# Expert rows loaded and turned in two tiles of half the turn's width, and the first pair's nearness products written five times over

## The chip, the cores and the metric

The kernel runs on one core of one Trainium2 chip. Each time is the device time of one execution in microseconds (us). The kernel before was run three times without a profile (764.43, 764.62 and 766.75 us, median 764.62) and once with one.

## The reference

Three stages follow each other, all in float32, over 1536 tokens of 512 numbers (2 batches of 768, 8 heads of 64):

```
q_assign = argmax(q_n . c_n);  k_assign = argmax(k_n . c_n)     # 16 centroids a head, unit vectors
attn     = softmax(q k^T / 8, only where q_assign == k_assign) @ v
x        = heads side by side, 1536 x 512
e        = argmax(xn . en / tau)          # one of 8 experts for each token
x        = gate * (relu(x @ w1[e]) @ w2[e])        # w1: 512 x 1024, w2: 1024 x 512
out      = ((x @ w_a) * (x @ w_b)) @ w_out         # 512 -> 1536 -> 512
```

## The kernel before, in words

**Attention** works on eight pairs of heads (four a batch), twelve steps a pair: `scores` (L620, L621) makes a 128 x 768 block of scores, `rowmax` (L629) its maximum on VectorE, `expo` (L634) the exponential on ScalarE, `etrans` (L652) turns the block on TensorE, `pv_gen` (L679) multiplies it with v. The cluster mask is a part of the scores' product: `prep_gen` finds each row's cluster and writes it as 16 further rows of the scores' operands `Q3` and `K3`.

**The first pair's preparation** (`prep_gen(0)`) has nothing to hide behind, since no scores can run before it. For head 0 it turns q and k (`turned`, L437), multiplies them with the 16 centroids in high and low halves, 32 columns for each tile of 128 rows (`near_c`, L449), adds the halves up on VectorE (L450), finds the maxima in a chain of VectorE instructions that ends with the one-hot tile `oh` (L491), and turns `oh` on TensorE (L554, tile `t2`), in three groups of four, between which the same products for head 1 stand (L449 again, six in each of two places). `near_c` runs for pair 0 alone; later pairs use `near_all` (L457). While TensorE would stand still there, `keep_warm` (L273) puts products of ones into a bank that nobody reads: six of 512 columns (`FL1`) stand ahead of the first group of L554. The instructions of an engine run in the order in which the code issues them; each engine waits for others by semaphores.

**Experts** (`layer1`, `layer2`). A scatter has put the rows of each expert into its own part of `xs_d` in HBM. There are eight turns, one an expert, with fixed widths (`WIDTHS` 256, 160, 256, 224, 248, 216, 192, 176): so many rows are computed in a turn. Turn 0 is gathered on the chip as the attention ends. For the turns 1 to 7 `load_xe` (L1194) fetches 256 rows, whatever the width, on ScalarE's DMA queue, as two tiles of 128 rows by 512, and `trans_x` (L1213) turns them with eight transposes of 128 columns into two PSUM banks, of which the first `WIDTHS` columns are copied out (L1218, L1222, L1224). A turn has eight blocks; `load_xe(e + 2)` is issued behind block 5 of turn e, and `trans_x(e + 1)` behind block 5 of turn e (block 6 in turn 0).

**Weights** stream all the while: `load_raw` (L159, SyncE's DMA queue) fetches 512 KB into one of four `raw` buffers, ScalarE rounds them (L210) and VectorE takes the rest (L213), which frees the buffer for the next fetch. ScalarE's casts stand in one queue with the relu of the blocks (L1309, L1316), so a cast that waits for its DMA holds the relu behind it.

**The last stage** (L1232, L1480) multiplies with `w_a`, `w_b` and `w_out`; neither part of the change touches it.

Of the kernel before, what the change touches and what calls it, by code (L numbers as in the profile page):

```python
# [9 lines left out]
F32 = mybir.dt.float32  # L10
# [12 lines left out]
P = 128  # L23
FAR = float(2.0 ** 100)
CAP = 256
WIDTHS = (256, 160, 256, 224, 248, 216, 192, 176)
# [17 lines left out]
FL6 = 3  # L44
STAND = {8: 4}
FL1 = 6
FL2 = 2
FL3 = 5

# [2 lines left out]
def kernel(  # L52
# [15 lines left out]
    nc = tc.nc  # L68
    B, H, S, D = q.shape
# [13 lines left out]
    CT = CAP // P  # L83
# [16 lines left out]
    xs_d = dram.tile([NE * RX, DM], F32, name="xs_d")  # L100
# [157 lines left out]
    identr = left.tile([P, P], F32R, name="identr")  # L258
# [11 lines left out]
    def keep_warm(ps, n):  # L270

        for _ in range(n):
            nc.tensor.matmul(ps.rearrange("p (a b) -> p a b", b=P), ones, ones.rearrange("p (o c) -> p o c", o=1).to_broadcast([P, 4, P]), start=True, stop=True)  # L273
# [40 lines left out]
    cbuf = att.tile([P, H, 7 * 2 * C], F32R, name="cbuf", bufs=1)  # L314
    own = slice(3 * 2 * C, 4 * 2 * C)
# [94 lines left out]
    def prep_gen(pp):  # L410

        a, c = rows_hl.pop(pp)
        Q2 = att.tile([P, 2 * S], F32R, tag="Q2", name=f"Q2_{pp}")
        K2 = att.tile([P, 2 * S], F32R, tag="K2", name=f"K2_{pp}")
# [4 lines left out]
        hp = pp % HP  # L419

        def bank(dt, name):
            return psa.tile([P, 512], dt, tag="rot", name=name, bufs=3)
# [17 lines left out]
        def near_c(hs, t0, t1, sv):  # L440
            slots = [2 * h + isk for h in hs for isk in range(2)]
            ns = len(slots)
            w = 2 * C
            pt = bank(F32, f"sm_{pp}_{t0}")
            for t in range(t0, t1):
                for i, sl in enumerate(slots):
                    h, isk = divmod(sl, 2)
                    o = ((t - t0) * ns + i) * w
                    nc.tensor.matmul(pt[:, o:o + w], (Q2, K2)[isk][:, h * S + t * P:h * S + (t + 1) * P], cbuf[:, 2 * hp + h, own], start=True, stop=True)  # L449
            nc.vector.tensor_reduce(out=sv[:, t0:t1].rearrange("p t s c -> p (t s) c"),  # L450
                                    in_=pt[:, :(t1 - t0) * ns * w].rearrange("p (a z c) -> p a c z", z=2, c=C), axis=AX.X, op=ALU.add)

# [52 lines left out]
        if pp == 0:  # L505
            for h in range(2):
                for dst, src in ((K2, c), (Q2, a)):
                    for g0 in (h * NT, h * NT + HALF):
                        turned(dst, src, g0, g0 + HALF)
                        if h:  # L510
                            next(firsts[0][3], None)
                        yield
                dup(slice(h * S, (h + 1) * S))
                svs[h] = new_sv((h,))
                if h == 0:
                    near_c((h,), 0, NT, svs[h])
                    first_of(h)
                    yield
# [17 lines left out]
        for hs, ns, ohs, fg in firsts:  # L536
# [5 lines left out]
            if pp == 0:  # L542
                h = hs[0]
                order = [(1, t) for t in range(NT)] + [(0, t) for t in range(NT)]
                for u in range(0, len(order), 4):
                    if h == 0 and u:
                        near_c((1,), (0, HALF)[u > 4], (HALF, NT)[u > 4], svs[1])
                    elif h == 0:
                        keep_warm(wps[:, :512], FL1)
                    pt = bank(F32, f"t2_{pp}_{u}")  # L550
                    if h:
                        keep_warm(pt, FL2 if u else FL3)
                    for j, (isk, t) in enumerate(order[u:u + 4]):
                        nc.tensor.matmul(pt[D:D + C, j * P:(j + 1) * P], oh[:, t, isk, :], identb, start=True, stop=True)  # L554
                    for isk in (1, 0):
                        js = [j for j in range(4) if order[u + j][0] == isk]
                        if not js:
                            continue
                        src = pt[D:D + C, js[0] * P:(js[-1] + 1) * P]
                        c0 = h * S + order[u + js[0]][1] * P  # L560
                        dst = (Q3, K3)[isk][D:, c0:c0 + len(js) * P]
                        if isk and u:
                            nc.scalar.activation(dst, src, AF.Copy, scale=FAR, bias=-FAR)
                        elif isk:
                            nc.vector.tensor_scalar(out=dst, in0=src, scalar1=-1.0, scalar2=FAR, op0=ALU.add, op1=ALU.mult)
                        else:
                            evac(dst, src)

                    if u + 4 < len(order):
                        yield  # L570
            elif pp == 1:
                R = ns * C
                ohT = att.tile([R, NT, P], F32R, tag="ohT", name=f"ohT_{pp}", bufs=1)
                pt = psa.tile([P, 1024], BF16, tag="rot", name=f"t2_{pp}", bufs=3)[:R, :NT * P]
                for j in range(NT):
                    nc.tensor.matmul(pt[:, j * P:(j + 1) * P], oh[:, j].rearrange("p s c -> p (s c)"), identb, is_transpose=True, start=(j == 0), stop=(j == NT - 1))
                src = pt.rearrange("p (b i) -> p b i", i=P)
# [5 lines left out]
            else:  # L583
                pt = bank(F32, f"t2_{pp}")[:, :NT * ns * C]
# [314 lines left out]
    for s in range(nst):  # L899
        g_, h, t = steps[s]  # L900
        pp = g_[0]
        i = s % SPP
# [6 lines left out]
        if s >= SPP and zeros:  # L909
            dst, src = zeros.pop(0)  # L910
# [150 lines left out]
    def new_x(key, dt=F32R):  # L1061
        return big.tile([P, 2, DC, CAP], dt, tag="xT", name=f"xT_{key}", bufs=2)
# [8 lines left out]
    key, cap, held, over, obase, pbase = (left.tile([P, 1, NE], F32, name=n) for n in ("key", "cap", "held", "over", "obase", "pbase"))  # L1071
# [119 lines left out]
    def load_xe(e):  # L1191
        t = big.tile([P, CT, DM], F32R, tag="xe", name=f"xe_{e}", bufs=2)
        at_row = nc.values_load(turn_i[0:1, NE + e:NE + e + 1], engines=[mybir.EngineType.Activation], min_val=RX, max_val=(NE - 1) * RX)
        i = nc.scalar.dma_start(out=t.bitcast(F32), in_=xs_d[bass.ds(at_row, CAP), :].rearrange("(c p) d -> p c d", p=P))  # L1194
        if e == 1:
            for o in scatters:
                tc.add_manual_dep(i.ins, o.name, DATA, reason="rows of every scatter")
        xe_t[e] = t
# [3 lines left out]
    def turn_bank():  # L1202
        ring[0] += 1
        return ("et0", "et1", "pp", "pv")[(ring[0] - 1) % 4]

    def trans_x(key, src):

        x = new_x(key, F32 if KINDS[key] == "one" else F32R)
        hi, lo = x[:, 0], x[:, 1]
        pts = [ps_t.tile([P, 2, CAP], F32R, tag=turn_bank(), name=f"xT_{key}_{u}") for u in range(2)]  # L1210
        for t in range(CT):
            for j in range(DC):
                nc.tensor.transpose(pts[j // 2][:, j % 2, t * P:(t + 1) * P], src[:, t, j * P:(j + 1) * P], identr)  # L1213
        pts = [p.bitcast(F32) for p in pts]
        wd = WIDTHS[key]
        if KINDS[key] == "one":
            for u in range(2):
                (nc.vector.tensor_copy if u else nc.scalar.copy)(hi[:, 2 * u:2 * u + 2, :wd], pts[u][:, :, :wd])  # L1218
            xT_t[key] = x
            return  # L1220
        for u in range(2):
            nc.scalar.copy(hi[:, 2 * u:2 * u + 2, :wd], pts[u][:, :, :wd])  # L1222
        for u in range(2):
            nc.vector.tensor_sub(lo[:, 2 * u:2 * u + 2, :wd], pts[u][:, :, :wd], hi[:, 2 * u:2 * u + 2, :wd])  # L1224
        xT_t[key] = x
# [273 lines left out]
    for G in range(total_f + tot + LAG):  # L1499
# [10 lines left out]
        if I < 0:  # L1510
            layer1(G)
            if G in (2, NF - 1):
                load_xe(1 if G == 2 else 2)
            if G == NF:
                further()
            if G == GR - 2:
                tc.mark_branch_hint_location("rare", "LikelyTaken", engines=[mybir.EngineType.DVE])
            e, f = divmod(G, NF)
            if 2 * NF <= G < 3 * NF:
                next(rr, None)  # L1520
            if G > 3 * NF:
                next(gg, None)
            if f == (5 if e else NF - 2):
                if e + 1 < NE:
                    trans_x(e + 1, xe_t[e + 1])
            if f == 5 and 0 < e < NE - 2:
                load_xe(e + 2)
        elif I < tot:
            bil1(I)
            next(pg_, None)  # L1530
# [52 lines left out]
```

## Time and profile before

| what | value |
|---|---|
| runs without a profile | 764.43, 764.62, 766.75 us |
| profiled execution | 765.42 us, of which the span from first to last instruction is 763.9 us |
| TensorE | busy 750.4 us, 98% of the span |
| VectorE, ScalarE | busy 464.3 us (61%) and 374.3 us (49%) |
| mean granted TensorE clock | 0.997 |

A share of the clock of 1.00 stands for 2.4 GHz, 0.50 for 1.2 GHz. "PEld" is the loading of the array's weights, which overlaps the products on "PE". A row of the timeline that ends in [x <-engine tile line] tells how long the engine stood idle before it and who released it.

### The profile page before, as it was taken

The numbers are of one execution on the slowest core, as the hardware profiler recorded it, in microseconds if no ns is written. First come the engines' busy times: TensorE is split into PE (matmuls) and PEld (weight loads), VectorE is DVE, ScalarE is ACT, GpSimd is POOL, SyncE is SP. The second block draws the span as 40 slices with busy tenths as digits, with TensorE's granted clock in tenths as the row PEclk, the third lists the DMA queues.
The fourth block names the chain that finished last, engine by engine and source line by source line (L and its number), as shares of the span: only waits on it lengthen the run. The fifth ranks groups of instructions, "written<-read, shape, count | busy, mean of one in ns | idle before, by whom it ended". The sixth has DMA issues, their size and how long they took to land.

```text
span 763.9 us, 12711 instructions
## 1 busy us (share of the span) xinstructions
PE 750.4 (98%) x4788; PEld 629.7 (82%) x4788; DVE 464.3 (61%) x912; ACT 374.3 (49%) x770; POOL 106.3 (14%) x145
## 2 busy tenths in 40 slices
PE   8999999999999999999999999999999999999996
PEld 5767777777777679998999999888898888888995
DVE  6877676787867677478876898677643121121211
ACT  4656766777676675366655565344332121111211
POOL 6303203051300041000000004122001020000201
PEclk9999999999999999999999999999999999999999
DMA  6327133161321026889879877554401010000100
GB/s 189 84 87 252 43 95 90 59 195 58 91 52 32 28 97 231 313 283 298 285 240 279 276 220 219 121 146 111 137 7 52 1 56 0 1 1 0 56 1 28
DMA packets 47747, 91.86 MB, mean 120 GB/s; under 512 B 6264, under 2 KB 19832, under 8 KB 47680
## 3 DMA queue, kind: packets, MB, share of 16 engines
q1 hardware_dynamic: 43472, 81.01, 35.5%
q0 software_dynamic: 2304, 6.31, 2.2%
q10 hardware_dynamic: 1904, 3.67, 1.4%
q8 instruction: 39, 0.64, 0.4%
q14 instruction: 28, 0.23, 0.1%
HBM read 69.27 MB, written 14.04 MB: 109 GB/s over the span
## 4 chain that ended last, share of the span: by engine, by line
issue 28%; PE 26%; DMA 3%; DVE 1%; POOL 1%; ACT 1%; POOLq 0%; SPq 0%; ACTq 0%; DVEq 0%
PE ab L1232 7%; PE y L1349 5%; PE y L1353 3%; PE h L1313 3%; PE h L1232 2%; DMA raw<-in_moe_w_dram 2%; PE h L1305 2%; PE o_sc L1480 1%; PE h L1314 1%; PE y L1354 1%; POOL out_dram L1458 1%; DVE w L213 1%; PE o_pp L1480 1%; PE o_pv L1480 1%; ACT w L210 1%
## 5 line engine op out<-in xcount | busy, mean ns | idle before, releaser
L1436 DVE TENSOR_TENSOR ga<-ab,ga 128x256 f32<-128x256 f32 (+1 forms) x48 | 26.7, 557 | 156.7 <-PE ab L1232 110.9
L634 ACT ACTIVATE E<-sc,nmx 128x768 f32<-128x768 f32 x96 | 86.8, 904 | 53.9 <-DVE nmx L629 46.7
L1232 PE MATMUL ab<-xT_b,w 128*128 128x256 f32 (+1 forms) x720 | 113.1, 304 | 0.0
L1232 PE MATMUL ab<-x,w 128*128 128x512 f32 x432 | 108.1, 390 | 0.0
L1232 PEld LDWEIGHTS ab<-xT_b,w 128*128 128x128 f32 x720 | 98.6, 190 | 7.2
L629 DVE TENSOR_REDUCE nmx<-sc 128x1 f32<-128x768 f32 x96 | 91.4, 953 | 6.8 <-PE sc L621 5.6
L1232 PEld LDWEIGHTS ab<-x,w 128*128 128x128 f32 x432 | 81.1, 188 | 17.2
L652 PEld LDWEIGHTS et<-ident,E 128*128 128x128 f32 x576 | 62.3, 140 | 32.4 <-ACT ET L656 12.8
L1435 ACT COPY ga<-ab 128x256 f32<-128x256 f32 (+1 forms) x48 | 23.1, 481 | 126.9 <-PE ab L1232 123.7
L652 PE MATMUL et<-ident,E 128*128 128x128 f32 x576 | 82.4, 279 | 1.6 <-ACT E L634 1.2
L658 DVE COPY ET<-et 128x384 f32<-128x384 f32 x96 | 52.6, 548 | 50.5 <-PE et L652 50.3
L620 PE MATMUL sc<-K,Q 80*128 80x512 f32 x192 | 73.0, 380 | 0.0
L679 PE MATMUL pv<-ET,v 128*64 128x384 f32 (+2 forms) x408 | 72.3, 479 | 0.3 <-DVE xrow L699 0.2
L213 DVE TENSOR_TENSOR w<-raw,w 128x1024 fp32r<-128x1024 f32 x48 | 58.1, 1218 | 19.3 <-ACT w L210 18.8
L1480 PE MATMUL o_sc<-w,g 128*128 128x512 f32 x288 | 69.5, 390 | 0.0
L1437 ACT CAST g<-ga 128x256 fp32r<-128x256 f32 (+1 forms) x48 | 24.7, 514 | 84.2 <-DVE ga L1436 84.2
L1480 PEld LDWEIGHTS o_sc<-w,g 128*128 128x128 f32 x288 | 53.9, 188 | 11.3
L621 PE MATMUL sc<-K,Q 128*128 128x512 f32 x192 | 61.3, 340 | 0.0
L1349 PE MATMUL y<-hh,w 128*128 128x256 f32 (+3 forms) x416 | 59.2, 290 | 0.0
L210 ACT CAST w<-raw 128x1024 fp32r<-128x1024 f32 x47 | 49.4, 1053 | 16.3 <-DMA raw<-in_moe_w_dram 12.3
L1349 PEld LDWEIGHTS y<-hh,w 128*128 128x128 f32 x416 | 54.4, 190 | 0.3 <-DVE ys L1323 0.3
L656 ACT COPY ET<-et 128x384 f32<-128x384 f32 x96 | 45.7, 476 | 2.7 <-PE et L652 2.7
(277 smaller groups left out, 1206.9 us busy)
## 6 DMA issues: line engine op xcount, KB each, us to landing
raw<-in_moe_w_dram SPq DMA_DIRECT2D x48, 512.0 KB, 5.1
w<-in_moe_w_dram SPq DMA_DIRECT2D x16, 512.0 KB, 9.7
raw<-in_moe_w_a_dram SPq DMA_DIRECT2D x12, 512.0 KB, 5.1
raw<-in_moe_w_b_dram SPq DMA_DIRECT2D x12, 512.0 KB, 4.5
raw<-in_moe_w_out_dram SPq DMA_DIRECT2D x12, 512.0 KB, 3.6
xs_d<-zero SPq DMA_DIRECT2D x8, 512.0 KB, 6.4
xe<-xs_d ACTq DMA_DIRECT2D x7, 512.0 KB, 6.5
v<-in_v_dram SPq DMA_DIRECT2D x8, 384.0 KB, 3.1
```

The source lines that it names most:

```text
L210: (nc.scalar.copy if late is None else nc.vector.tensor_copy)(hi, w)
L213: nc.vector.tensor_sub(lo, w, hi)
L620: nc.tensor.matmul(ps[:, lo:hi], Q3[:, qs], K3[:, h * S + lo:h * S + hi], start=True, stop=False)
L621: nc.tensor.matmul(ps[:, lo:hi], Q2[:, qs], K2[:, h * S + lo:h * S + hi], start=False, stop=True)
L629: nc.vector.tensor_reduce(out=nmx[pp][:, h, t:t + 1], in_=sc[s], axis=AX.X, op=ALU.max, negate=True)
L634: nc.scalar.activation(e, sc.pop(s), AF.Exp, bias=nmx[pp][:, h, t:t + 1], accum_out=sums[pp][:, t, h:h + 1])
L652: nc.tensor.transpose(pt[:, j * P:(j + 1) * P], e[:, kt * P:(kt + 1) * P], ident)
L658: nc.vector.tensor_copy(dst, src)
L679: nc.tensor.matmul(pv[h * D:(h + 1) * D, :], vt[:, h, kt, :], ets[g, h][:, kt, :n * P], start=(kt == 0), stop=(kt == NT - 1))
L1232: nc.tensor.matmul(ps, s_, m_, start=(i == 0), stop=(i == len(ops) - 1))
L1349: nc.tensor.matmul(ys_ps[e][j // 2][:, j % 2, :wd], w[:, m_, ff, j * P:(j + 1) * P], s_, start=(f == 0 and i == 0 and j % 2 == 0), stop=(l ...
L1480: nc.tensor.matmul(o_ps[ck][t], s_[:, t * P:(t + 1) * P], w_[:, m_], start=(f == 0 and i == 0), stop=(J == I and f == NF2 - 1 and i == 2))
```

## The change

`near_c`: each product writes 160 columns in place of 32, the same 32 five times side by side (`AGAIN`). The next product begins 32 columns further on and writes over the four copies, so that what L450 reads stays the same; the last one of a bank ends at column 512, the bank's end. There are 24 such products.

`load_xe` and `trans_x`: with h half the turn's width, the rows come as two tiles of h rows, 2 h in place of 256 rows, and the transposes take h rows by 128 and write h columns each. The h of the turns 1 to 7 are 80, 128, 112, 124, 108, 96 and 88.

```diff
+AGAIN = 5
...
-                    nc.tensor.matmul(pt[:, o:o + w], (Q2, K2)[isk][:, h * S + t * P:h * S + (t + 1) * P], cbuf[:, 2 * hp + h, own], start=True, stop=True)
+                    nc.tensor.matmul(pt[:, o:o + AGAIN * w].rearrange("p (a c) -> p a c", c=w), (Q2, K2)[isk][:, h * S + t * P:h * S + (t + 1) * P],
+                                     cbuf[:, 2 * hp + h, own].rearrange("p (o c) -> p o c", o=1).to_broadcast([cbuf.shape[0], AGAIN, w]), start=True, stop=True)
...
-        i = nc.scalar.dma_start(out=t.bitcast(F32), in_=xs_d[bass.ds(at_row, CAP), :].rearrange("(c p) d -> p c d", p=P))
+        h = WIDTHS[e] // CT
+        i = nc.scalar.dma_start(out=t[:h].bitcast(F32), in_=xs_d[bass.ds(at_row, CT * h), :].rearrange("(c p) d -> p c d", p=h))
...
+        h = WIDTHS[key] // CT
...
-                nc.tensor.transpose(pts[j // 2][:, j % 2, t * P:(t + 1) * P], src[:, t, j * P:(j + 1) * P], identr)
+                nc.tensor.transpose(pts[j // 2][:, j % 2, t * h:(t + 1) * h], src[:h, t, j * P:(j + 1) * P], identr[:h, :h])
```

No engine gets an instruction more or less, or another order; shapes change alone. On TensorE, in the first pair's preparation (sm is the tile of the nearness products, t the turned rows, wps the bank of the warming products), before:

```order
L449 MATMUL sm_0_235<-cbuf,Q_0_185 128x32
L449 MATMUL sm_0_235<-cbuf,K_0_186 128x32
...
L437 MATMUL t_0_6_253<-identr,kr_169 128x128 x3
L437 MATMUL t_0_9_261<-identr,kr_169 128x128 x3
L437 MATMUL t_0_6_268<-identr,qr_168 128x128 x3
L437 MATMUL t_0_9_274<-identr,qr_168 128x128 x3
```

and now, its lines numbered one or two higher:

```order
L451 MATMUL sm_0_235<-cbuf,Q_0_185 128x160
L451 MATMUL sm_0_235<-cbuf,K_0_186 128x160
...
L438 MATMUL t_0_6_253<-identr,kr_169 128x128 x3
L438 MATMUL t_0_9_261<-identr,kr_169 128x128 x3
L438 MATMUL t_0_6_268<-identr,qr_168 128x128 x3
L438 MATMUL t_0_9_274<-identr,qr_168 128x128 x3
```

Only the last number of the products moved, from 32 to 160.

On ScalarE's queue, behind block 5 of turn 2, where the rows of turn 4 are fetched between the casts of two weight buffers (hh is the relu, xT the turned rows of turn 3, w the rounded weights), before:

```order
L1222 CAST xT_5619<-xT_1_5621 128x2x224
L1194 DMA xe_5634<-xs_d 128x2x512
L210 CAST w_5594<-raw_5511 128x1024
L1309 ACTIVATE hh_5662<-h_5663 128x256
L210 CAST w_5690<-raw_5556 128x1024
```

and now:

```order
L1227 CAST xT_5619<-xT_1_5621 128x2x224
L1198 DMA xe_5634<-xs_d 124x2x512
L211 CAST w_5594<-raw_5511 128x1024
L1314 ACTIVATE hh_5662<-h_5663 128x256
L211 CAST w_5690<-raw_5556 128x1024
```

The transfer keeps its place and goes over 124 partitions in place of 128.

On TensorE, behind block 6 of turn 0, where turn 1 is turned, before and then now:

```order
L1232 MATMUL h_5113<-xT_3559,w_3623 128x256 x12
L1213 MATMUL xT_0_5129<-identr,xe_3654 128x128 x2
L1213 MATMUL xT_1_5130<-identr,xe_3654 128x128 x2
...
L1349 MATMUL y_0_3667<-hh_5030,w_3713 128x256 x2
L1349 MATMUL y_1_3668<-hh_5030,w_3713 128x256 x2
```

```order
L1237 MATMUL h_5113<-xT_3559,w_3623 128x256 x12
L1218 MATMUL xT_0_5129<-identr,xe_3654 128x80 x2
L1218 MATMUL xT_1_5130<-identr,xe_3654 128x80 x2
...
L1354 MATMUL y_0_3667<-hh_5030,w_3713 128x256 x2
L1354 MATMUL y_1_3668<-hh_5030,w_3713 128x256 x2
```

The eight transposes stand where they stood and write 80 columns each.

## Rows read from the trace of the kernel before

**Rows 1.** The page: busy us, share of the span and instructions of each engine.

```profile
PE 750.4 (98%) x4788; PEld 629.7 (82%) x4788; DVE 464.3 (61%) x912; ACT 374.3 (49%) x770; POOL 106.3 (14%) x145
```

**Rows 2.** TensorE's waits over the span: us in total, times, longest.

```profile
PE h L1232 <- DVE hh L1310: 1.7, 1, 1.7
```

**Rows 3.** Stretches: length, busy us (instructions) of each engine, PEclk, DMA share, GB/s.

```profile
5.00:9.00 4.00, 3.39 (x24) 1.82 (x22) 2.65 (x12) 2.47 (x8) 1.33 (x4) 1.00 0.95 294
9.00:10.30 1.30, 1.30 (x13) 1.30 (x13) 0.91 (x1) 0.36 (x1) 1.00 (x1) 1.00 0.86 173
11.70:14.30 2.60, 2.60 (x8) 0.69 (x6) 1.16 (x4) 2.25 (x4) 1.02 (x1) 0.50 0.77 182
```

**Rows 4.** Timeline of the preparation: start, us, engine, line, operation.

```profile
7.38 0.25 DVE L321 TENSOR_SCALAR csq<-cent_sb,c_r 128x64 f32<-128x64 f32 x1
7.78 0.44 PE L325 MATMUL pc<-ident,csq 128*64 128x128 f32 x4 [0.46 <-DVE csq L321]
11.68 2.73 PE L273 MATMUL wps<-ones 128*128 128x512 bf16 x6
12.68 0.36 DVE L491 TENSOR_TENSOR oh<-smm,mx 128x192 bf16<-128x192 f32 x1
14.34 0.60 PE L554 MATMUL t<-identb,oh 128*16 128x128 bf16 x4
15.75 0.39 PE L554 MATMUL t<-identb,oh 128*16 128x128 bf16 x4
16.84 0.39 PE L554 MATMUL t<-identb,oh 128*16 128x128 bf16 x4
18.68 1.90 PE L273 MATMUL kw<-ones 128*128 128x512 bf16 x8
```

**Rows 5.** Timeline: two products of 32 columns, two of 256 columns.

```profile
9.48 0.26 PE L449 MATMUL sm<-cbuf,K 128*128 128x32 f32 x1
9.60 0.26 PE L449 MATMUL sm<-cbuf,Q 128*128 128x32 f32 x1
...
17.74 0.28 PE L620 MATMUL sc<-K,Q 80*128 80x256 f32 x1
17.86 0.29 PE L621 MATMUL sc<-K,Q 128*128 128x256 f32 x1
```

**Rows 6.** Transposes: eight and what follows; weight loads by line, ns min/median/max.

```profile
304.94 0.80 PE L1213 MATMUL xT<-identr,xe 128*128 128x128 f32 x8
305.57 1.67 PE L1349 MATMUL y<-hh,w 128*128 128x256 f32 x12
L1213 PEld LDWEIGHTS xT<-identr,xe x56: 137/140/143, 304.8 to 431.0; 128*128 128x128 f32 x56
L376 PEld LDWEIGHTS pe__756<-ident,en x4: 132/137/138, 51.7 to 51.9; 8*128 8x128 f32 x4
```

**Rows 7.** Transfers: ScalarE's queue over the span; all packets from 0 to 30 us.

```profile
q10 hardware_dynamic: 1904, 3.67, 1.4%
DMA packets 2834, 4.01 MB, mean 134 GB/s; under 512 B 520, under 2 KB 2568, under 8 KB 2832
```

**Rows 8.** Stretches of the experts, columns as in rows 3.

```profile
321.00:324.00 3.00, 3.00 (x28) 3.00 (x27) 2.17 (x3) 2.90 (x5) 0.00 (x0) 1.00 0.47 150
357.00:360.00 3.00, 3.00 (x24) 2.92 (x23) 2.37 (x4) 1.99 (x6) 0.00 (x0) 1.00 0.91 307
```

**Rows 9.** Timeline around TensorE's one wait, and behind it.

```profile
347.89 1.05 ACT L210 CAST w<-raw 128x1024 fp32r<-128x1024 f32 x1 [1.55 <-DMA raw<-in_moe_w_dram]
348.85 0.38 ACT L1309 ACTIVATE hh<-h 128x256 fp32r<-128x256 f32 x1
350.58 1.69 PE L1232 MATMUL h<-xT,w 128*128 128x256 f32 x12 [1.68 <-DVE hh L1310]
358.13 0.39 DVE L1318 SCALAR_TENSOR_TENSOR hh<-hf,hh 128x224 fp32r<-128x224 f32 x1
360.20 0.37 PE L1353 MATMUL y<-hh,w 128*128 128x448 f32 x1
```

## The prediction

> **What bounds the kernel now.** I read the busy time of the engines first. TensorE is busy 98% of the span [rows 1]: time comes off where TensorE waits or where its work shrinks, and any work added in its queue may cost. Then TensorE's waits: one stands out, 1.68 us before a layer 1 product at 350.58 [rows 2, 9]. Last, the granted clock by stretches, since busy time hides a slow clock: 1.00 from 5 to 10.3 us, and 0.50 (1.2 GHz) from 11.7 to 14.3 [rows 3]. So there are three places to look at: the first 17 us, the seven turnings, and the weight stream about 350 us. The change puts wider products into the first, fewer columns into the second, and fewer rows but another cut of the transfer into the third.
>
> **The wide products, taken by themselves.** The 32-column products follow each other every 0.12 us (9.48, 9.60), and so do two of 256 columns (17.74, 17.86) [rows 5]: the time between two hardly depends on columns up to there, so 160 columns cost nothing, 24 times. Below nothing is excluded, since no instruction goes; above, the last one's columns could delay VectorE's sum behind it by some 0.05 us, three times. I take 0. No wait is added: SyncE's, ScalarE's and GpSimd's queues get nothing here.
>
> **What they may change is the clock.** Before it fell, TensorE had not stood still: it was busy 1.30 of 1.30 us from 9.0 to 10.3, with the twelve narrow products, against 3.39 of 4.00 in the stretch before, with transposes and 512-column products, behind which the clock had stayed [rows 3]. What differs is what ran, and the change makes five times the columns run there. The rows don't tell what the clock goes by; that it stays up now is my likeliest case and no more.
>
> If it stays, two pieces shorten. First, the six warming products ahead of the first group of L554: they start at 11.68 and take 2.73 us, so that L554 starts at 14.34, though the one-hot tile it needs is done at 12.68 + 0.36 = 13.04 [rows 4]. At the full clock eight of the same kind take 1.90 us, 0.24 each at most [rows 4]; six end their turn at 11.68 + 6 x 0.24 = 13.1, so what is late next is `oh`. From VectorE's end to TensorE's start the pair csq (7.63) and pc (7.78) has 0.15 us, which puts L554 at 13.04 + 0.15 = 13.19: 14.34 - 13.19 = 1.15 us sooner. Second, the first round of L554 and six nearness products takes 15.75 - 14.34 = 1.41 us, the second, the same work behind the clock's return, 16.84 - 15.75 = 1.09 [rows 4]: 0.32 us. Together -1.47. VectorE's next steps wait for TensorE there, so all of it moves up, the scores too; with TensorE at 98% afterwards, nothing behind takes it back. Ends: 0 (the clock falls just the same) and -1.5; I take -1.5.
>
> **The transposes.** Eight take 305.57 - 304.94 = 0.63 us, 0.079 each [rows 6]. Half a width is 80 to 128; the sum of (1 - h/128) over seven turns is 1.25. If time went with columns, the gain would be 1.25 x 0.63 = 0.79 us. If the weight loads set it, nothing: a load takes 140 ns with 128 rows and 137 with 8 rows [rows 6], so fewer rows don't shorten it. That excludes a loss too. The load row is the nearer one; I take -0.1.
>
> The Trainium skill has a rule here ("TensorE: Matmul & The Clock Gate", section "LDWEIGHTS (loading the stationary operand)"): a load takes the columns of the weights over 1.2 GHz, which for 128 columns is an estimate of 107 ns and would hide all that the moving side saves. The pairs here follow each other every 79 ns, under that figure, so the measurement decides and the loads aren't the whole of it. By that rule this term is 0, by the other end 0.79.
>
> **Fewer rows fetched.** 1472 in place of 1792 rows of 2 KB, 640 KB less. That can help only at the one stall: ScalarE's cast at 347.89 had waited 1.55 us for a weight buffer, the relu stood behind it until 348.85, and TensorE until 350.58 [rows 9]. Turn 1's transfer (192 KB less) comes long before, and in between, from 321 to 324, the DMA engines were busy for 0.47 only [rows 8], so its gain is spent. Turn 3's saves 64 KB; at 307 GB/s [rows 8] that is 0.2 us. Ends: 0 and the whole stall, -1.7. I take -0.2.
>
> **Another cut of the transfers.** ScalarE's queue has 1904 packets for seven transfers [rows 7], 272 each: 256 rows and 16 tails, one an engine, so 16 rows an engine. From 0 to 30 us 520 packets are under 512 B [rows 7]. The centroids and tau have 128 each, which leaves 264 tails for 17 transfers, 16 x 16 + 8: the one over 8 partitions (`emb_sb`) used 8 engines. So the cut is in equal whole shares. 80, 128, 112 and 96 partitions divide by 16; 124 divides at most by 4, 108 by 12, 88 by 11. Turn 4's transfer, issued right behind the cast at 347.89, would then put 248 / 4 = 62 rows on each of four engines, 46 more than now. A packet takes 763.9 x 16 x 0.014 / 1904 = 0.09 us [rows 7], so this is 46 x 0.09 = 4.1 us more on four engines, in a stretch where all are at 0.91 [rows 8] and a weight buffer is whole only when its slowest engine is done. What hides it: its own use comes a turn later, and if packets of the two queues alternate, a weight buffer's 16 packets there wait for 16 others, 16 x 0.09 = 1.4 us. The relu's second half ends at 358.52 and its product starts at 360.20 [rows 9], 1.7 us of cover. Turn 5's (18 rows an engine) adds 0.2 us under the same cover, turn 7's none. Ends: 0 and +4.1; I take +0.3.
>
> **Sum.** -1.5 - 0.1 - 0.2 + 0.3 = -1.5. The profiled execution took 765.42 us (span 763.9 and 1.5 around it), 0.8 over the median of 764.62; no row tells whether the runs without a profile had the same fall of the clock. I set the sum against the median: 763.1 us.
>
> **The rivals.**
> - *The clock falls all the same*, or fell only in the profiled execution. For: TensorE was wholly busy before the fall and it came. Against: the wide products are the one difference to the stretch before. Left are -0.1 - 0.2 + 0.3: 764.6.
> - *Turn 4's transfer holds the weight stream.* On four engines the weight packets stand behind the 62, not between them: 4.1 us late, less the cover of 1.7 is 2.4 us of TensorE's idle time about 355 to 362, and with it the castings queue up before the relu as at 347.89. It decides from 1.7 us of lateness on. With the startup's gain: 764.6 - 1.8 + 2.4 = 765.2, and 766.9 where no cover is left: slower than before. For: ScalarE already waits for weights there. Against: queues may alternate.
>  The Trainium skill states this cut ("DMA: Bandwidth & Descriptors", section "Why a DMA increments its semaphore by 16 and not by 1"): a transfer uses the largest number of engines up to 16 that divides the partitions. By that rule 124 go over 4; the trace agrees for 8 partitions, and none of before has 124.
> - *Both small terms come whole.* The transposes give 0.8 and the stall at 350.58 goes, 1.7: 764.6 - 1.5 - 0.8 - 1.7 = 760.6, with half of each 761.9. For: a load lasts 140 ns and a pair takes 79 [rows 6], so loads overlap and something else may set the pace. Against: the idle DMA engines from 321 to 324.
>
> **How the numbers follow.** What a measurement of this kernel can tell from no change is about 0.3%, 2.3 us: 762.3 and 766.9. Forecast 0.50, with a range of its own from 762.1 to 764.2; clock falls 0.22, stream held 0.14, small terms whole 0.14. Faster: the third rival and a fifth of the forecast, 0.14 + 0.10 = 0.24. Slower: half of the second rival, 0.07. Same: 0.69. The range leaves out the ends of the last two rivals: 761.7 to 765.7.
>
> **What would show it.** The clock at 1.00 from 11.7 to 14.3 and the first L554 near 13.2: right; at 0.50, the first rival. The nearness products still 0.12 us apart. Eight transposes of turn 1 under 0.55 us would mean that columns count. ScalarE's queue with 1472 rows and 16 x 4 + 4 + 12 + 11 = 91 tails, 1563 packets, would show the uneven cut, 1584 an even one. An idle time of TensorE between 352 and 362, released by VectorE, the second rival. The forecast is wrong if the median leaves 762.1 to 764.2, and its first step is wrong if the clock stays and the third group of L554 still starts at 16.84.

## The result, and the profile after

The changed kernel took 772.07 us (median of 6 runs, 770.18 to 773.85), the kernel before 764.52 beside it (6 runs, 762.90 to 766.75): a ratio of 1.0092, 95% interval 1.0077 to 1.0107. That is 7.5 us slower. The forecast was 763.1 with a range up to 765.7: it was wrong, and on the other side.

The page of the changed kernel: span, the engines' line (VectorE, ScalarE and GpSimd stand within 0.7 us of [rows 1]), and ScalarE's DMA queue with packets, MB and share.

```profile
span 771.4 us, 12709 instructions
PE 752.9 (98%) x4788; PEld 632.1 (82%) x4788; DVE 465.0 (60%) x912; ACT 374.2 (49%) x770; POOL 106.3 (14%) x145
q10 hardware_dynamic: 1563, 3.02, 1.3%
```

The share of TensorE is still 98%. The span went from 763.9 to 771.4, while its busy time grew by 2.5 us only, so some 5 us are idle time. The queue's 1563 packets are the count that the prediction gave for the uneven cut: 1472 rows and 91 tails.

TensorE's waits, with us in total, times, longest. They answer to [rows 2].

```profile
PE y L1358 <- DVE hh L1323: 3.5, 1, 3.5
PE h L1237 <- ACT xT L1138: 1.4, 1, 1.4
PE y L1358 <- ACT ys L1367: 0.9, 1, 0.9
PE h L1237 <- DVE hh L1315: 0.8, 1, 0.8
```

The wait of before, 1.7 us on `hh` at 350, is down to 0.8. A new one, 3.5 us in one piece, stands ahead of a layer 2 product of turn 3. Its place is read in the timeline (start, us, engine, line, operation, idle time before and its releaser); the lines answer to [rows 9].

```profile
348.72 0.52 ACTq L1198 DMA_DIRECT2D xe<-xs_d  x1
352.85 1.05 ACT L211 CAST w<-raw 128x1024 fp32r<-128x1024 f32 x1 [0.74 <-DMA raw<-in_moe_w_dram]
360.59 1.04 ACT L211 CAST w<-raw 128x1024 fp32r<-128x1024 f32 x1 [6.41 <-DMA raw<-in_moe_w_dram]
361.55 0.35 ACT L1321 ACTIVATE hh<-h 128x224 fp32r<-128x224 f32 x1
363.23 0.39 DVE L1323 SCALAR_TENSOR_TENSOR hh<-hf,hh 128x224 fp32r<-128x224 f32 x1
363.77 0.44 PE L1358 MATMUL y<-hh,w 128*128 128x448 f32 x1 [3.54 <-DVE hh L1323]
365.50 0.74 PE L1358 MATMUL y<-hh,w 128*128 128x448 f32 x1 [0.87 <-ACT ys L1367]
371.32 0.28 PE L1359 MATMUL y<-hh,w 128*128 128x224 f32 x1
```

Read it backwards. TensorE waits for VectorE, VectorE for ScalarE's relu, and the relu stands in ScalarE's queue behind a cast that waited 6.41 us for a weight buffer. The same cast ran at 355.49 in the kernel before, so the buffer is 5.1 us late. The product came at 360.20 then [rows 9] and comes at 363.77 now: 3.57 us late, 1.53 of the 5.1 were hidden.

The rest of the 7.5 us lies behind the stall. In these stretches the columns are length, busy us (instructions) of TensorE, PEclk, DMA share, GB/s.

```profile
360.00:364.40 4.40, 0.86 (x6) 1.00 0.60 149
364.50:371.30 6.80, 5.93 (x21) 0.50 0.65 241
```

TensorE was busy for 0.86 of 4.40 us, and then the clock stood at 0.50 (1.2 GHz) for 6.8 us. At 371.32 the product on line 1359 is 7.46 us behind its twin of the kernel before, and that lag stays to the end. So 3.57 us are the stall and 3.9 what came behind it, a second short wait of 0.87 among them.

The two steps at which the change aimed did come. The clock by stretches, all engines shown (answers to [rows 3]), and TensorE's timeline of the preparation (answers to [rows 4, 5]) of the changed kernel:

```profile
9.00:10.30 1.30, 1.27 (x11) 1.27 (x12) 0.78 (x1) 0.49 (x2) 1.02 (x1) 1.00 0.67 165
11.70:14.30 2.60, 2.60 (x20) 1.58 (x19) 1.94 (x5) 2.37 (x5) 0.83 (x1) 1.00 0.69 173
```

```profile
11.86 1.47 PE L274 MATMUL wps<-ones 128*128 128x512 bf16 x6
13.27 0.39 PE L557 MATMUL t<-identb,oh 128*16 128x128 bf16 x4
13.77 0.28 PE L451 MATMUL sm<-cbuf,K 128*128 128x160 f32 x1
13.88 0.27 PE L451 MATMUL sm<-cbuf,Q 128*128 128x160 f32 x1
15.58 0.39 PE L557 MATMUL t<-identb,oh 128*16 128x128 bf16 x4
```

The clock is 1.00 where it was 0.50. The wide products follow each other every 0.11 us, the narrow ones did every 0.12. The first one-hot group starts 1.07 us sooner, the third 1.26.

### The profile page after: what moved, and what is told of

Its sections match the earlier page's. It is cut to its first block, busy times and chain, and to the rows that moved or that the text cites. A ratio compares the mean times of both kernels' runs of the same rounds, so it can differ in the third digit from the quotient of the medians.

```text
span 771.4 us, 12709 instructions
## 1 busy us (share of the span) xinstructions
PE 752.9 (98%) x4788; PEld 632.1 (82%) x4788; DVE 465.0 (60%) x912; ACT 374.2 (49%) x770; POOL 106.3 (14%) x145
## 3 DMA queue, kind: packets, MB, share of 16 engines
q10 hardware_dynamic: 1563, 3.02, 1.3%
## 4 chain that ended last, share of the span: by engine, by line
issue 28%; PE 25%; DMA 4%; DVE 2%; POOL 1%; ACT 1%; POOLq 0%; SPq 0%; DVEq 0%; ACTq 0%
PE ab L1237 7%; PE y L1354 4%; DMA raw<-in_moe_w_dram 3%; PE y L1358 3%; PE h L1318 2%; PE h L1237 2%; PE h L1310 2%; PE o_sc L1485 1%; PE y L1359 1%; DVE w L214 1%; PE h L1319 1%; POOL out_dram L1463 1%; PE o_pp L1485 1%; PE o_pv L1485 1%; DMA res<-tab_d 0%
```

## The experiments

Eleven kernels ran besides the changed one. Each time is a median beside runs of the kernel before on the same chip, with the ratio and its 95% interval.

**The two parts apart.** First the products alone: before, with line 449 as the change has it.

```
+AGAIN = 5
-nc.tensor.matmul(pt[:, o:o + w], ..., cbuf[:, 2 * hp + h, own], ...)
+nc.tensor.matmul(pt[:, o:o + AGAIN * w]..., cbuf[...].to_broadcast([cbuf.shape[0], AGAIN, w]), ...)
```

> The wide nearness products alone, expert rows as before. In the changed kernel TensorE was 1.3 us ahead of before from 13.8 us to 287 us, and not ahead at 288.5, where turn 0 begins. Theory A (the startup's gain is real, what took it back at turn 0 comes from the half-width rows or is chance): 1.3 us under before, some 763.2, with turn 0's first product near 287.2. Theory B (something at turn 0 takes the lead back, whatever the rows): TensorE ahead by 1.3 until 287 and level at 288.5, time within 0.5 us of before. Theory C (the clock held by chance in that one profile): the clock falls between 11 and 16 us again and the time is that of before.

763.92 us (12 runs) against 764.13, ratio 0.9996, 0.9985 to 1.0007. Its profile has the clock at 1.00 from 11.7 to 14.3 and a span 0.8 us shorter; the loss isn't here.

Then the half-width rows alone: the changed kernel with the narrow product back.

> The half-width rows alone, nearness products of 32 columns as before. Theory A (all the loss is the rows'): time of the changed kernel or up to 1.3 us over it, 772 to 773.5, with TensorE idle 3 us or more between 355 and 366 and the clock at half behind it. Rival (the loss needs both parts, since the earlier start moved turn 4's transfer against the weights): within 1 us of before, 764.5.

770.54 us (4 runs), 1.0081, 1.0059 to 1.0102. The whole loss is in this part. Its waits of TensorE and its half clock:

```profile
PE y L1357 <- DVE hh L1322: 2.8, 1, 2.8
```

```profile
366.70:370.10 3.40, 3.40 (x13) 3.13 (x13) 3.06 (x7) 2.83 (x7) 0.00 (x0) 0.50 0.57 175
```

**Turn 4 alone, and all but turn 4.** The first takes before and cuts turn 4 into halves of 124 rows, the other six turns staying at 128; the second takes the changed kernel and puts turn 4 back to 128. The same edit stands in `trans_x`.

```
-h = WIDTHS[e] // CT
+h = WIDTHS[e] // CT if e == 4 else P     # turn 4 alone, narrow products
+h = WIDTHS[e] // CT if e != 4 else P     # all but turn 4
```

> Before, with turn 4 alone fetched and turned as two tiles of 124 rows; all other turns 128 rows as before. Theory A (one transfer, cut over four engines, is the whole loss): as much over before as the half-width rows alone, some 772, with its packets lasting 12 us and 4 tails on that transfer. Rival (the loss is the sum over the uneven turns 4, 5 and 7, or the transposes): under half of that, below 768.

> The changed kernel, but turn 4 fetched and turned as two tiles of 128 rows. Theory A (turn 4's transfer is the whole loss): 764.5 or less, down to 762.8 if the startup's gain comes through; no idle time of TensorE over 2 us and no half clock behind 340 us. Rival (turns 5 and 7, over 12 and 11 engines, hold the stream too): 766 or more, with an idle time of TensorE behind 380 or 425 us.

Turn 4 alone: 771.88 us (4 runs), 1.0098, 1.0076 to 1.0120, the whole loss, by an edit that fetches 8 of 256 rows less. All but turn 4: 764.42 (12 runs), 1.0004, 0.9990 to 1.0019, no loss that can be measured, though turns 5 and 7 still go over 12 and 11 engines. ScalarE in the kernel with turn 4 alone shows the mark of the changed kernel, a cast that waits some 6 us:

```profile
353.55 1.05 ACT L211 CAST w<-raw 128x1024 fp32r<-128x1024 f32 x1 [0.92 <-DMA raw<-in_moe_w_dram]
360.81 1.04 ACT L211 CAST w<-raw 128x1024 fp32r<-128x1024 f32 x1 [5.93 <-DMA raw<-in_moe_w_dram]
```

**How the transfer holds the stream.** The queues' packets, MB and share in the same 12 us, 351 to 363, of the kernel before (with its weight fetches and their median from issue to landing) and then of the changed one; q1 carries the weights, q10 the rows:

```profile
q1 hardware_dynamic: 1551, 3.00, 75.0%
q10 hardware_dynamic: 263, 0.51, 12.0%
raw<-in_moe_w_dram SPq DMA_DIRECT2D x6, 512.0 KB, 5.0
```

```profile
DMA packets 1310, 2.56 MB, mean 213 GB/s; under 512 B 70, under 2 KB 70, under 8 KB 1308
q1 hardware_dynamic: 1058, 2.03, 65.2%
q10 hardware_dynamic: 250, 0.51, 16.4%
```

The row packets are about as many as before, the weights' fell from 1551 to 1058, six fetches issued to four. Turn 4's transfer took 12.1 us (350.98 to 363.09) in place of 3.0 (350.81 to 353.78). On four engines its 248 rows are 62 each.

A fetch of weights ends with 16 small packets (under 512 B), one an engine, so these tell how far the engines are. First the kernel before and the changed kernel from 354.0 to 355.4, ahead of the cast that starts at 355.49 before; then the changed kernel from 352.5 to 360.2, where the same cast starts at 360.59:

```profile
DMA packets 164, 0.32 MB, mean 227 GB/s; under 512 B 16, under 2 KB 16, under 8 KB 163
```

```profile
DMA packets 148, 0.29 MB, mean 209 GB/s; under 512 B 12, under 2 KB 12, under 8 KB 147
```

```profile
DMA packets 960, 1.90 MB, mean 247 GB/s; under 512 B 40, under 2 KB 40, under 8 KB 958
q10 hardware_dynamic: 169, 0.35, 18.7%
```

Before, all 16 engines end the buffer in this time. Now 12 end it and four do not, and the 40 up to 360.2 are 3 x 12 + 4: twelve engines were through with their shares of three buffers when the other four were through with the first. Meanwhile 169 row packets passed, 42 on each of the four, beside the 16 weight rows and the one tail of that buffer. So the two queues did not go one for one there; why the rows were ahead isn't shown. This is worked out from counts; no view gives a record by engine.

The buffers behind the first were held as long as it was. The first profile of the changed kernel has no landings for them, but a second one, told of below, has three fetches issued from 349.0 to 353.7, which landed 8.9, 8.7 and 9.4 us after their issue (4.6 to 5.4 in the kernel before). Their line, with the median:

```profile
raw<-in_moe_w_dram SPq DMA_DIRECT2D x3, 512.0 KB, 8.9
```

**Two transfers.** The changed kernel, with the rows of an uneven half fetched in two: a multiple of 16 partitions, and the rest.

```
-dma_start(out=t[:h], in_=src[:h])
+g = h // 16 * 16
+for p0, p1 in ((0, g), (g, h)): dma_start(out=t[p0:p1], in_=src[p0:p1])
```

> The changed kernel, with each uneven half fetched by two transfers, the largest multiple of 16 rows and the rest (112 + 12, 96 + 12, 80 + 8): the same rows, the same transposes. Theory A (the number of engines is what counts, not the rows or the turning of 124 rows): no loss, 763 to 764.5, turn 4's first transfer with 16 tails and done in 4 us. Rival (tiles of 124 rows cost by themselves, in the turning or by 24 fewer even packets): 768 or more.

766.06 us (12 runs), 1.0020, 1.0007 to 1.0032. Some 6 of the 7.5 us are gone with the same rows, columns and transposes: the cut decides, not the size. Turn 4's two took 3.1 us (350.54 to 353.59). About 1.3 us over the kernel before remain. The further issue in ScalarE's queue may be their price, but nothing was run on it, and the profile, with a span of 763.7 against 763.9 before, shows no loss.

**Warm through the stall.** The changed kernel, with 14 warming products of the startup's kind queued ahead of turn 3's first layer 2 product, where TensorE stands still.

```
 ys_ps[e] = [...]
+if e == 3:
+    keep_warm(ys_ps[e][0]..., 14)
```

> The changed kernel with 14 warming products of 512 columns (some 3.0 us at the full clock) ahead of turn 3's first layer 2 product, where TensorE stood idle for 3.5 us. Theory A (the loss has two parts, the stall of 3.5 and the half clock that follows it, which took 3.9 us): the clock stays at 1.00 behind 360 us, 768 to 768.7. Rival (the clock falls whatever runs in the stall, or the later half of the loss is the weight stream's own): 771 or more, the half clock or further waits behind 364 us.

770.12 us (4 runs), 1.0090, 1.0059 to 1.0122: not to be told from the changed kernel. In the profile, though, the clock stayed up, and the span was 767.5, 3.9 under 771.4. Two single executions can differ by nearly as much (the six of the changed kernel spread over 3.7 us), so the changed kernel and this one ran again beside each other:

> The changed kernel once more, on the chip of the next run, as the other end of that comparison: 770 to 774. If the half clock behind the stall is in the runs without a profile too, this one stands some 3 us over the next.

> The changed kernel with 14 warming products ahead of turn 3's first layer 2 product, as before, timed beside the unwarmed one. If the half clock behind the stall is a cost of its own (6.8 us at 0.50 in the profile, 3.9 us of lag), this is 2 to 4 us under the changed kernel of the same call, 768 to 770.5. If the clock fell in the profiled execution alone, or the warming products cost as much as they save, the two are equal within 1 us.

770.96 us (6 runs, 768.08 to 773.00) and 769.40 (6 runs, 767.88 to 772.59), ratios 1.0088 (1.0059 to 1.0117) and 1.0078 (1.0051 to 1.0105). The second profile of the changed kernel spans 768.0 us, so the 3.9 between the first two profiles were mostly not the warming. The same stretch as above, of the second run of the warmed kernel (all engines), and the stall's place in it:

```profile
364.50:371.30 6.80, 6.80 (x49) 6.53 (x48) 6.70 (x13) 5.17 (x12) 0.00 (x0) 1.00 0.82 266
```

```profile
358.41 3.20 PE L274 MATMUL y<-ones 128*128 128x512 bf16 x14
361.26 0.56 PE L1360 MATMUL y<-hh,w 128*128 128x448 f32 x1
```

Every run has its mean granted clock: 0.991 to 0.997 over the six of the changed kernel, mean 0.9943, and 0.997 to 0.998 warmed, mean 0.9977. The half clock is thus in the runs without a profile too, and 0.0034 x 769 = 2.6 us of full speed are lost to it on average. The times differ by 1.6 in the medians and 0.9 in the means, with intervals that overlap: my 2 to 4 us are not shown. The second kernel spends the stall's time in the warming products, and no wait for `hh` is left behind them, so they may have taken back a part.

**The same cut where the stream isn't late.** Before, with turn 5 alone fetched as halves of 124 rows, again on four engines (`h = 124 if e == 5 else P`).

> Before, with turn 5 alone fetched as two tiles of 124 rows (more than its width of 216 needs; only the first 216 are used), so that the transfer over four engines stands one turn later. Theory A (any such transfer in the weight stream holds it, some 5 us less the cover of 1.7): 767 to 772, with an idle time of TensorE between 374 and 386 us. Rival (it hurt in turn 4 alone, since ScalarE's casts were already waiting for weights there): under 766.

764.74 us (10 runs), 1.0003, 0.9981 to 1.0024: no loss that can be measured. The transfer took 9.1 us (375.37 to 384.46), and of the four weight fetches issued from 375 to 385 the one whose landing is on record took 9.9 us from issue to landing, against a median of 4.3 in the kernel before. TensorE did not wait for it:

```profile
raw<-in_moe_w_dram SPq DMA_DIRECT2D x4, 512.0 KB, 9.9
```

```profile
12.40:22.60 10.20, 10.20 (x41) 6.82 (x40) 5.35 (x11) 3.50 (x8) 6.60 (x4) 0.50 0.63 166
374.00:386.00 12.00, 12.00 (x92) 11.68 (x91) 8.35 (x18) 6.89 (x14) 0.00 (x0) 1.00 0.87 250
```

TensorE is busy 12.00 of 12.00 us. The same slow transfer cost nothing there, where the buffers were far enough ahead; in turn 4's place the casts were waiting for weights already [rows 9]. The first row is told of at the end.

**Versions without the uneven cut.** One halves only turns 1, 2, 3 and 6, whose halves divide by 16; one rounds each half up to a multiple of 16.

```
+h = WIDTHS[e] // CT if WIDTHS[e] % 32 == 0 else P   # even halves only
+h = -(-WIDTHS[e] // 32) * 16                        # rounded up
```

> The changed kernel with half-width tiles only where the half divides by 16 (turns 1, 2, 3 and 6); turns 4, 5 and 7 as tiles of 128 rows. Theory A (12 and 11 engines cost nothing that can be measured): the same as with turn 4 alone put back, 763.5 to 764.8. Rival (turns 5 and 7 cost too): 1 us or more under that.

> The changed kernel with each half rounded up to a multiple of 16 rows (128, 80, 128, 112, 128, 112, 96, 96), the wide nearness products kept. If the four engines of turn 4's transfer are the cause, every transfer is cut into 16 shares again (256 rows an engine's worth in equal shares, 16 tails each), nothing is late at 355 to 362, and the time is that of the kernel with turn 4 alone put back: 762.5 to 765, no loss against before. If fewer rows or smaller transposes as such cost, it stays over 766.5. A gain over 0.3% would need the startup's 1.1 us and the wait at 350 together; I do not expect it to be measurable.

765.29 us (12 runs), 1.0004, 0.9992 to 1.0016, and 764.69 (12 runs), 1.0000, 0.9985 to 1.0015. Both lose nothing and win nothing. In the second all seven transfers are even again, 1504 rows and 7 x 16 tails, and the wait of before is back to 1.4 us:

```profile
q10 hardware_dynamic: 1616, 3.08, 1.3%
```

```profile
PE h L1237 <- DVE hh L1315: 1.4, 1, 1.4
```

No version beats both kernels by more than can be measured.

## Why the prediction was wrong

**The step that failed is "Another cut of the transfers", "I take +0.3".** The cut itself was right: 1563 packets, four tails in turn 4's transfer, 62 rows on each of four engines. The Trainium skill's rule ("DMA: Bandwidth & Descriptors", section "Why a DMA increments its semaphore by 16 and not by 1") agrees with all that ran: 124 partitions left 4 tails, 108 left 12, 88 left 11, and 80, 96, 112 and 128 left 16.

What failed is what was made of it. "If packets of the two queues alternate, a weight buffer's 16 packets there wait for 16 others, 1.4 us" was set against the cover of 1.7, and the term taken at 0.3. The queues did not alternate so: by the counts above the first buffer's share on the four engines stood among 42 row packets, and its cast came 5.1 us late. The buffers behind it, already under way, were held as long. The term's own upper end, 4.1, was the nearer value, and nothing in the rows spoke for less. It was still low: 42 + 17 packets in the 7.7 us from 352.5 to 360.2 are some 0.13 us each, an estimate from these counts, where the prediction had 0.09.

**The second rival, at 0.14, is what came,** and it too was too small. It had the weights standing behind the 62, 4.1 us late, and 2.4 us of idle time at 355 to 362; they were 5.1 late, and the stall is 3.57, at 360 to 364. Its cover of 1.7 was nearly right, 1.53 measured. Its price left out what stands behind a stall: the clock at 0.50 for 6.8 us, in the profile 3.9 us with the short wait there. The prediction read the clock as a matter of the first 17 us alone, though [rows 3] had shown one fall and so the price of another. With what this profile measured, 5.1 - 1.5 + 3.9, the term is 7.5, the whole loss; the second profile, with shorter waits and 3.4 us of half clock, spans 3.4 us less.

**The startup was right in its mechanism and not in its worth.** The clock stays up, the groups start 1.07 and 1.26 us sooner (1.15 and 1.47 were forecast). "Nothing behind takes it back" failed in this profile: the wait on `xT` at turn 0, 1.4 us above, was 0.2 in the kernel before, and at 288.5 the two kernels stand level. What releases it there isn't in the records, but it was that one execution's: in the second profile of the changed kernel the wait is 0.2 again, and turn 0's first product starts at 287.31, 1.21 us sooner than the 288.52 of before. The products alone kept their 0.8 us to the end of their profile. In runs without a profile that kernel's gain lies between 1.1 us and a loss of 0.5. The clocks of the runs say why it is small: mean 0.9980 over 12 runs with the wide products, 0.9973 over the 23 of the kernel before beside them, 0.0007 x 764 = 0.5 us. Six of those 23 have 0.999, which leaves no room for a fall as the profiled one had (its clock is 0.997). So the profiled execution showed a fall that only some runs have; the prediction named that doubt and then set the gain whole against the median.

**The other two rivals** did not come: the clock didn't fall at the start, and the small terms didn't come whole. **The wide products by themselves** cost nothing, as taken.

**The transposes** were right. In the changed kernel's timeline the eight of turn 1, at 80 rows and columns, take 305.62 - 305.02 = 0.60 us against 0.63:

```profile
305.02 0.77 PE L1218 MATMUL xT<-identr,xe 80*128 80x80 f32 x8
305.62 1.58 PE L1354 MATMUL y<-hh,w 128*128 128x256 f32 x11
```

By that row turn 1, the narrowest, gives 0.03, and seven turns 0.1, as taken.

**Fewer rows fetched** can't be read alone. The wait at 350 is 0.8 in the changed kernel, 1.7 with the halves alone, 1.4 rounded up, 1.9 with even halves, and none with all but turn 4. It varies by up to 1.9 us among kernels that fetch the same rows up to there, so 0.2 us can't be found in it, and the kernel without the wait is not measurably faster than the one before.

## What to carry to other kernels

Count the engines that a transfer's partitions are cut over before trimming them: 248 rows on four engines cost more than 256 on sixteen, and padding to a multiple of 16 cost nothing. Price a slow transfer by all the packets that its few engines have to pass before the next buffer is whole, not by an even turn-taking of two queues that nothing has shown, and look whether the stream beside it has anything in hand: here the same cut was free one turn later. A stall on TensorE can have a second price in the clock behind it: here it had in every profile of a kernel with the slow transfer in turn 4, unless warming products filled the stall.

## What the runs showed of the hardware that was not expected

- Behind the stall the granted clock was 0.50 for 6.8 us in the changed kernel and 3.4 us in the one with the halves alone; with warming products in the stall it stayed at 1.00. Shorter single waits, 1.4 to 1.9 us (rounded up, even halves), had no fall behind them; the changed kernel run again, with two of 1.9 and 1.0 us within 360 to 364, had a mean of 0.61 from 364.5 to 368.
- With nearness products of 32 columns the clock fell at the start in all four profiles, among them for 10.2 us (12.4 to 22.6) in the kernel with turn 5 cut; with 160 columns in none of nine. TensorE was busy nearly throughout in both cases, as the rows from 9.0 and 11.7 us show. What it goes by stays open.
- The DMA share hid the trouble: 0.88 in the kernel before and 0.82 in the changed one from 351 to 363, while the rate fell from 294 to 213 GB/s.
